# Block-sparse attention with a gated FFN: a plan computed while building against a written-out order of all pieces

## The chip, the core and the metric

The program runs on one core of one Trainium2 chip. The metric is device time in microseconds; three runs of the kernel before gave 344.5 to 351.38 with a median of 347.37. One more execution was profiled. Engines are named as in the profile: PE (TensorE matmuls), PEld (its weight loads), DVE (VectorE), ACT (ScalarE), POOL (GpSimd) and SP (SyncE, which here only issues DMAs and reads registers). POOL issues DMAs too, on a queue of its own.

## The reference

Attention with 4 batches, 8 heads, 768 positions of 64 numbers, cut into 24 blocks of 32 positions. A query block sees its neighbours, the first and the last block, and three blocks drawn for it (`sampled_blocks`); the first and last query blocks see everything. The output goes through a gated FFN with three matrices.

```python
mask = np.abs(blk_i - blk_j) <= 1
mask = mask | (blk_i == 0) | (blk_j == 0) | (blk_i == n_blocks - 1) | (blk_j == n_blocks - 1)
for qb in range(n_blocks):
    for kb in sampled_blocks[qb]:
        mask[qb*block:(qb+1)*block, kb*block:(kb+1)*block] = True
attn = softmax(np.where(mask, q @ k.T / sqrt(D), -1e9))     # per batch and head
x = (attn @ v).transpose(0, 2, 1, 3).reshape(B * S, H * D)  # 3072 x 512
out = (x @ w_gate -> sigmoid) * (x @ w_val) @ w_out         # d_ff = 1536, float32 out
```

## The kernel before, in words

**Pieces.** The kernel is a list of about 1400 pieces of a few instructions, each with an engine (or a choice of two), a duration, what it depends on, and the buffers that it takes and gives back. Names are a kind, the batch, and a number:

- `cdma`, `memset`, `mask`, `gv0`, `gc0`: constants, the block numbers, the mask row and the first and last block of batch 0's values.
- `ldv`, `ldk`, `ldq` (lines 564 to 579): loads of a batch's values, keys and queries by POOL's queue, converted to f16 on the way. In batch 0 the keys come in two halves (`ldk00`, `ldk01`), the queries in a first part of 64 rows and a second of 32 (`lda00`, `ldb00`).
- `trk`, `trq` with `evk`, `evq`: transposes of keys and queries on PE, and their copies out of PSUM. `rrk`, `rrq` (line 689) rearrange them on POOL first, from batch 1 on.
- `vsh` (line 738) rearranges the values on DVE, `scr` (746, 750) writes them to DRAM, and SP gathers from there: `w` (822) the neighbour blocks of a window of query blocks into V1A to V1D, `vg` (873) the three drawn blocks of one query block into V2A to V2D with three DMAs, whose addresses are registers. `regSP` and `regPOOL` (611) load these registers from `vidx` and `kidx`. `vfl` (787) fills the first and last block into the same buffers.
- `kfl` and `kg` (801, 858): POOL copies the fixed and the drawn key blocks together.
- For each pair of query blocks: `sc` (scores, 899 and 907), `mx` (row maximum, 917), `ex` (exponential, two halves, 927), `rz` (936), `sl` (normalisation, two halves: 948 on DVE or 945 on POOL), `tp` (transposes, 960), `te` (copy, 966), `pv` (probabilities by values, 978, and 983 in batch 0), `xe` (copy into the FFN's input). The first and last query blocks have the same with a `d` ahead: `dsc`, `dmx`, `dex`, `dsl`, `dtp`, `dte`, `dpv`, `dxe`.
- FFN, in nine groups of 1, 1, 2, 2, 2, 4, 4, 4 and 4 tiles of 128 tokens: for each of 12 slices `pg` and `pu` (gate and value matmuls, 1146), `th` (tanh, 1155), `h` (1160); then for each tile `py` (1173), `ys` (1182), `st` (the store). `wg`, `wv` and `wo` (589, 597) are the weights' loads on POOL's queue, in three chunks each: slices 0 to 3 need `wg0` and `wv0`, 4 to 7 `wg1` and `wv1`, the rest `wg2` and `wv2`.

**What sets the order.** `Planner.run` (from line 283) plays the pieces through on the durations given, takes at each step the piece with the lowest priority number among those that could start first, and gives it engine and buffers; `TUNE` holds the numbers, with some 180 offsets (`off`) by kind and batch. The order that comes out is the program's order, and each engine works through its own in that order. `sl` of batches 0 and 1 may only go to DVE, of batch 2 only to POOL, of batch 3 to either.

**Idle matmuls.** Until bank 7 of PSUM is first used, the emitting loop puts matmuls of zeros (WZ, line 1204) where the plan has PE waiting, as many as 0.9 of the planned gap holds. There are 91 of them.

**The start.** SP issues the block numbers, a table of block indices (`bb_cst`), the identity, and `gv0`. POOL clears WZ and other tiles, then issues the loads in the order `ldk00 ldk01 lda00 ldv00 ldb00 wg0 wv0`. DVE forms `kidx`, `vidx` and then the mask (13 more small instructions) as one piece, on which the register loads depend. PE begins with `trk000 ... trk003, trq000 ... trq003, dsc0_0, trq010 ... trq013, sc0_4, sc0_6`.

## Time and profile before

| | |
|---|---|
| median of three runs | 347.37 us |
| profiled execution | 350.14 us, span 348.3 us |
| PE busy | 323.6 us (93%), 65.3 us of it in line 1173, 25.6 us in idle matmuls (line 1204) |
| DVE, ACT, POOL busy | 239.0, 192.5, 130.5 us |
| granted clock of PE over the span | 0.985 |
| DMA | 42.26 MB in 43169 packets |

How to read it: "busy" is the time in which an engine had an instruction running; the ends of matmuls are modelled, and an idle matmul counts like any other. The granted clock is the share of full speed that PE was given. `SPq` and `POOLq` are the queues of instructions that issue DMAs or read registers. A row of the chain is start, length and what ran or was waited for; a row of a stretch is its bounds and length, then busy time and instructions by engine, the granted clock, the DMA engines' mean share and GB/s. A row of the order of time is start, length, engine, line, operation, and what wrote what; rows of DMA issues end with the size of each and the median us from issue to landing.

### The profile page before, as it was taken

What the parts mean: (1) busy time and instruction counts of PE and PEld (TensorE: products, weight loads), DVE (VectorE), ACT (ScalarE), POOL (GpSimd) and SP (SyncE); (2) the same over time, 40 slices, a digit from 0 to 9 for tenths busy, and PEclk for the clock granted to TensorE, in tenths of its full rate; (3) what the DMA queues carried; (4) which work ended last, traced back from release to release, by engine and by line L of the source; (5) the groups of instructions that cost most, each with busy time, mean ns of one, the idle gap of its engine ahead of it and who ended that gap; (6) DMA issues with size and microseconds to landing.
All of it is one profiled execution on the core that took longest, in us unless ns stands there. A gap on an engine that the chain in (4) does not pass through costs nothing.

```text
span 348.3 us, 13695 instructions
## 1 busy us (share of the span) xinstructions
PE 323.6 (93%) x5227; PEld 205.9 (59%) x5227; DVE 239.0 (69%) x516; ACT 192.5 (55%) x588; POOL 130.5 (37%) x364
## 2 busy tenths in 40 slices
PE   8979669699989989689999999999999999999995
PEld 3446448586767678378565665665556555544442
DVE  4788568661798979469998788587777679703320
ACT  2464356524676577377676554665774667424321
POOL 7946115104304434234827894465241222000000
PEclk9999998979999999999999999999999999999999
DMA  7987983997331359952349943531313412020002
GB/s 125 207 193 146 242 193 73 213 219 159 118 103 44 117 115 202 203 178 79 83 135 206 212 115 94 161 106 47 89 31 121 139 49 81 14 90 30 2 30 90
DMA packets 43169, 42.26 MB, mean 121 GB/s; under 512 B 6592, under 2 KB 39936, under 8 KB 43008
## 3 DMA queue, kind: packets, MB, share of 16 engines
q1 hardware_dynamic: 28912, 27.23, 25.9%
q0 software_dynamic: 14192, 14.16, 25.5%
q8 instruction: 41, 0.67, 0.8%
q14 instruction: 24, 0.20, 0.2%
HBM read 46.08 MB, written 9.44 MB: 159 GB/s over the span
## 4 chain that ended last, share of the span: by engine, by line
PE 64%; DMA 15%; DVE 9%; issue 3%; ACT 3%; SPq 3%; POOL 2%; POOLq 0%; DVEq 0%; ACTq 0%
PE pall L1146 29%; PE pall L1173 16%; DMA stg<-in_q_dram 5%; PE pall L960 4%; PE pall L978 4%; DMA stg<-in_v_dram 4%; SPq L873 3%; PE pall L907 2%; DMA V1D<-scr 2%; DVE HT L1160 2%; DVE NM L917 2%; DMA scr<-XL 2%; DVE P L948 2%; PE pall L899 2%; DMA V2D<-scr 2%
## 5 line engine op out<-in xcount | busy, mean ns | idle before, releaser
L927 ACT ACTIVATE P<-pall,NM 128x256 f16<-128x256 f32 x176 | 81.4, 473 | 18.5 <-DVE NM L917 14.7
L1160 DVE SCALAR_TENSOR_TENSOR HT<-TH,pall 128x512 f16<-128x512 f32 (+2 forms) x108 | 54.3, 505 | 46.0 <-PE pall L1146 41.2
L858 POOL COPY KG<-KT 128x64 f32 x264 | 50.8, 241 | 84.4 <-PE pall L907 80.3
L1155 ACT ACTIVATE TH<-pall 128x512 f32<-128x512 f32 (+2 forms) x108 | 48.8, 455 | 57.6 <-PE pall L1146 50.5
L1173 PE MATMUL pall<-wo,HT 128*128 128x512 f16 x288 | 65.3, 379 | 0.2
L917 DVE TENSOR_REDUCE NM<-pall 128x4 f32<-128x1024 f32 x44 | 53.6, 1220 | 12.7 <-PE pall L907 7.5
L1146 PE MATMUL pall<-XT,wv 128*128 128x256 f16 (+2 forms) x336 | 57.2, 295 | 2.1 <-DVE HT L1160 1.4
L1146 PE MATMUL pall<-XT,wg 128*128 128x256 f16 (+2 forms) x336 | 56.8, 293 | 1.2 <-DVE HT L1160 1.0
L1146 PEld LDWEIGHTS <-wv 128*128 128x128 f16 x432 | 38.3, 101 | 25.7 <-issue 4.2
L1146 PEld LDWEIGHTS <-wg 128*128 128x128 f16 x432 | 38.3, 100 | 23.9 <-issue 2.8
L1173 PEld LDWEIGHTS <-HT 128*128 128x128 f16 x288 | 27.4, 98 | 31.0 <-issue 1.1
L945 POOL TENSOR_TENSOR P<-P,ZZ 128x512 f16<-128x512 f16 x26 | 27.7, 1080 | 23.8 <-DVE ZZ L936 18.5
L927 ACT ACTIVATION_READ_ACCUMULATOR P<-pall,NM 128x1 f32 x176 | 36.2, 206 | 0.0
L948 DVE TENSOR_SCALAR P<-P,ZZ 128x256 f16<-128x256 f16 x124 | 32.6, 324 | 1.1
L1182 ACT ACTIVATE YS<-pall 128x512 f32<-128x512 f32 x16 | 9.6, 597 | 36.2 <-PE pall L1173 36.2
L966 DVE COPY PTS<-pall 128x1024 f16<-128x1024 f16 x39 | 26.6, 684 | 3.1 <-PE pall L960 3.0
L960 PE MATMUL pall<-ident,P 128*128 128x128 f16 x352 | 27.5, 223 | 0.6 <-DVE P L948 0.6
L1204 PE MATMUL pall<-WZ 128*128 128x512 f16 x91 | 25.6, 416 | 1.3 <-POOL ones L538 1.3
L960 PEld LDWEIGHTS <-P 128*128 128x128 f16 x352 | 22.4, 100 | 5.0 <-DVE P L948 0.8
L1146 PE MATMUL pall<-XL,wg 128*128 128x512 f16 x96 | 24.5, 379 | 0.1
L1146 PE MATMUL pall<-XL,wv 128*128 128x512 f16 x96 | 24.5, 379 | 0.0
L689 POOL COPY stg<-stg 96x2048 f32<-96x2048 f32 x6 | 11.3, 1889 | 28.4 <-DMA stg<-in_k_dram 21.5
(115 smaller groups left out, 443.9 us busy)
## 6 DMA issues: line engine op xcount, KB each, us to landing
out_dram<-YS SPq DMA_DIRECT2D x24, 256.0 KB, 2.0
stg<-in_v_dram POOLq DMA_DIRECT2D x4, 768.0 KB, 11.4
V2C<-scr SPq DMA_DIRECT2D x96, 32.0 KB, 3.1
V2D<-scr SPq DMA_DIRECT2D x78, 32.0 KB, 2.8
stg<-in_k_dram POOLq DMA_DIRECT2D x3, 768.0 KB, 12.4
stg<-in_q_dram POOLq DMA_DIRECT2D x3, 768.0 KB, 16.9
scr<-stg SPq DMA_DIRECT2D x12, 192.0 KB
V1C<-scr SPq DMA_DIRECT2D x5, 384.0 KB, 3.5
```

Of the source, the lines that this page charges most:

```text
L858: pin(nc.gpsimd.tensor_copy(t[:, :, u, (2 + n) * BLK : (3 + n) * BLK].bitcast(f32), KT[r].bitcast(f32)[:, :, bass.ds(regs[key][i, n], BLK ...
L917: pin(nc.vector.tensor_reduce(NM[o.slots[hz][1]][:, 0:4].rearrange("p (h u) -> p h u", h=2), t, axis=AX.X, op=ALU.max, negate=True))
L927: pin(nc.scalar.activation(pb[:, hh, u, :], t[:, hh, u * 256 : u * 256 + 256], AF.Exp, bias=NM[z][:, 2 * hh + u : 2 * hh + u + 1], scale=1 ...
L945: pin(nc.gpsimd.tensor_tensor(pb, pb, z[:, 2 * hh : 2 * hh + 2].unsqueeze(2).broadcast_to([128, 2, 256]), op=ALU.mult))
L948: pin(nc.vector.tensor_scalar(pb[:, u, :], in0=pb[:, u, :], scalar1=z[:, 2 * hh + u : 2 * hh + u + 1], scalar2=None, op0=ALU.mult))
L960: pin(nc.tensor.transpose(t[:, m * 128 : m * 128 + 128], pb[:, hh, u, c * 128 : c * 128 + 128], ident))
L966: pin(copy(o)(PTS[pl.handles[hTS][1]].rearrange("p m n -> p (m n)"), banks[pl.handles[hT][1]].bitcast(f16)))
L1146: pin(nc.tensor.matmul(t, wt[:, c, f_ * 128 : f_ * 128 + 128], XT[g][:, c, :], start=(c == 0), stop=(c == 3)))
L1155: pin(nc.scalar.activation(TH[o.slots[ht][1]][:, 0:n], banks[pl.handles[hg][1]][:, 0:n], AF.Tanh, bias=0.0, scale=0.5))
L1160: pin(nc.vector.scalar_tensor_tensor(HT[:, f_, hoff : hoff + n], in0=TH[pl.handles[ht][1]][:, 0:n], scalar=1.0, in1=banks[pl.handles[hv][1 ...
L1173: pin(nc.tensor.matmul(t, HT[:, f_, hoff + tt * 128 : hoff + tt * 128 + 128], wo[:, f_, :], start=(f_ == 0), stop=(f_ == NF - 1)))
L1204: pin(nc.tensor.matmul(banks[7], WZ[:, 0:128], WZ, start=True, stop=True))
```

## The change

1. `Planner.run` no longer plans: it reads a table, `ORDER`, in which every piece stands once, with its engine, the number of the buffer that it takes, and, behind a "+", the idle matmuls ahead of it. The offsets, margins and the 0.9 go; so do the planned gaps. There are 111 idle matmuls.
2. The table of block indices is counted by POOL (`iota`) in place of its DMA; WZ is cleared by DVE (`wz`) in place of POOL.
3. `kidx` and `vidx` are a piece of their own (`idx`), on which the register loads depend in place of `mask`. `gv0` is issued after `cdma`.
4. Batch 0 is loaded in the order values, two halves of keys, two parts of queries (`'first': 'vkab'`). `wg0` and `wv0` come after the first key gathers.
5. `sl` and `te` may go to either of two engines in every batch; the table says which. Durations of pieces are lower, which only the old planner read; names of the second part of the queries change (`trqb01...`).

The arithmetic of the other pieces is untouched.

```diff
- 'load': [4, 10, 7],
+ 'load': [17, 9, 9],
- 'gate': [-1, -1, 2, 3, 3, 6, 10, 13, 14],
+ 'gate': [-1, -1, 3, 3, 5, 5, 9, 9, 9],
- 'sl': ['D', 'D', 'P', 'PD'],
- 'te': ['D', 'DA', 'D', 'D'],
+ 'sl': ['PD', 'PD', 'PD', 'PD'],
+ 'te': ['DA', 'DA', 'DA', 'DA'],
- 'first': 'kavb',
+ 'first': 'vkab',
...
+ORDER = """
+wz:D memset:G cdma:S ldv00:G0 gv0:S ldk00:G3 ldk01:G lda00:G1 mask:D ldb00:G gc0:A vsh0:D0 vfl0D:D idx:D vfl0B:D
+regSP0_0:S regPOOL0_0:G trk001:P0+43 evk001:D scr0:S trk002:P0+7 trk000:P1 trk003:P3 evk000:A evk003:D evk002:A
+trq001:P0+5 kfl01:G trq000:P1 kfl00:G evq001:A trq002:P3 kg0_6:G1 evq000:A trq003:P2 evq002:D evq003:A kg0_4:G0
+sc0_6:P0+3 w0_4:S0 mx0_6:D1 vg0_6:S kfl02:G sc0_4:P3+1 kg0_8:G2 trqb011:P1 mx0_4:D6 ex0_60:A0 w0_8:S0 kg0_10:G0
+vg0_5:S ex0_61:A regPOOL0_1:G ex0_40:A1 rz0_6:D sc0_8:P0+9 sl0_61:D w0_16:S0 vg0_11:S mx0_8:D3 ex0_41:A wg0:G
+sc0_10:P3+5 rz0_4:D evqb011:D ex0_80:A2 wv0:G trqb012:P0 mx0_10:D5 vg0_7:S evqb012:A sl0_60:G trqb010:P0+2 sl0_41:D
+wg1:G tp0_6:P10+2 evqb010:D vg0_4:S vfl0A:D sl0_40:G ex0_100:A0 ex0_81:A kg0_12:G1 te0_6:A vfl0C:G sc0_12:P2+10
+trqb013:P0 ex0_101:A mx0_12:D2 tp0_4:P12 te0_4:D ex0_120:A1 vg0_8:S rz0_10:D rz0_8:D sl0_80:D sl0_81:G ex0_121:A
+dsc0_0:P02+6 dmx0_00:D0 w0_12:S0 sl0_100:G evqb013:A vg0_9:S pv0_4:P1+3 rz0_12:D dmx0_01:D7 dex0_00:A1 wv1:G
+tp0_8:P01 sl0_121:G te0_8:D xe0_4:A dex0_01:A0 pv0_6:P1+3 dsl0_00:D vg0_10:S kg0_18:G2 xe0_6:A dsl0_01:D
+dtp0_00:P00+2 sl0_101:D dsc0_23:P02 wg2:G dte0_00:D dtp0_01:P1 sl0_120:G dmx0_231:D4 dte0_01:A dmx0_230:D0 kg0_14:G0
+dex0_231:A1 tp0_12:P12+5 wv2:G dex0_230:A0 pg0_0:P00+1 pu0_0:P1 tp0_10:P00 wo0:G th0_0:A2 regSP0_1:S dsl0_230:D
...
+"""
...
-    ENG = ("PE", "ACT", "DVE", "POOL", "SP")
+    ENG = {"P": "PE", "A": "ACT", "D": "DVE", "G": "POOL", "S": "SP"}
-    def run(self, switch=0.095, dma_lat={"SP": 1.8, "POOL": 2.8}):
...
+    def run(self, table):
+        byname = {o.name: o for o in self.ops}
+        self.handles, self.whole = {}, {}
         order = []
+        for item in table.split():
+            item, _, idle = item.partition("+")
+            name, _, how = item.partition(":")
+            o = byname.pop(name)
+            o.eng, o.idle = self.ENG[how[0]], int(idle or 0)
+            for (h, options), c in zip(o.acq, how[1:]):
+                o.got[h] = self.whole[h] = options[int(c)]
+                o.slots[h] = self.handles[h] = options[int(c)][0]
...
             order.append(o)
...
-        pin(nc.sync.dma_start(cst_t, cst_h.ap()))
         pin(nc.sync.dma_start(ident, ident_h.ap()))
+    def f_wz(o):
+        pin(nc.vector.memset(WZ, 0.0))
     def f_memset0(o):
-        pin(nc.gpsimd.memset(WZ, 0.0))
         pin(nc.gpsimd.memset(ones, 1.0))
+        pin(nc.gpsimd.iota(cst_t, pattern=[[1, NB], [0, 3]], base=0, channel_multiplier=0, allow_small_or_imprecise_dtypes=True))
         pin(nc.gpsimd.memset(mrow, 0.0))
...
+    P("wz", "DVE", 0.3, f_wz, prio=-200)
+    def f_idx(o):
+        for t, n in ((vidx, BLK), (kidx, BLK // 2)):
+            pin(nc.vector.tensor_scalar(t, in0=flat[0:1], scalar1=n, scalar2=None, op0=ALU.mult))
     def f_mask(o):
-        pin(V.tensor_scalar(kidx, in0=flat[0:1], scalar1=BLK // 2, scalar2=None, op0=ALU.mult))
-        pin(V.tensor_scalar(vidx, in0=flat[0:1], scalar1=BLK, scalar2=None, op0=ALU.mult))
         pin(V.tensor_copy(rb.rearrange("p a b -> p (a b)"), flat))
...
+    o_idx = P("idx", "DVE", 0.3, f_idx, deps=[c_dma], prio=-101)
-                regop[key] = P(f"reg{eng}{b}_{part}", eng, 1.6, f_regs(eng, key, part), deps=[o_mask] + lastuse[eng], prio=pr - 3)
+                regop[key] = P(f"reg{eng}{b}_{part}", eng, 1.6, f_regs(eng, key, part), deps=[o_idx] + lastuse[eng], prio=pr - 3)
...
-    order = pl.run()
-        if warm and o.eng == "PE":
-            n = int((o.start - t_pe) * TUNE["warm"] / 0.2135)
-            for _ in range(n):
-                pin(nc.tensor.matmul(banks[7], WZ[:, 0:128], WZ, start=True, stop=True))
+    for o in pl.run(ORDER):
+        for _ in range(o.idle):
+            pin(nc.tensor.matmul(banks[7], WZ[:, 0:128], WZ, start=True, stop=True))
         if o.fn is not None:
             o.fn(o)
```

The rest of the table, as far as it is spoken of: of the pieces `sl1` it puts 15 of 22 on POOL, of `sl0` 11, of `sl2` 12, of `sl3` 10. POOL's order after the part shown is `wo0 kg0_16 regPOOL0_2 kg0_2 wo1 kg0_20 wo2 kg0_1 sl0_141 ldv10`, and around batch 2's queries `sl1_101 kg1_16 sl1_81 sl1_80 ldq20 kg1_18 ... rrq2`. On PE the second output tile `py1_0` comes after all eight transposes of batch 1 and `dsc1_0`; before, it came ahead of them. `trq201`, the first transpose of batch 2's queries, stands between `pg4_8` and `pg4_9`; `tp1_8` stands ahead of `py3_1`. In the last two groups the slices no longer run from 0 to 11 (`pg7_2 pg7_0 pg7_3 pg7_5 ...`, `pg8_8 pg8_1 pg8_9 ...`).

## The prediction

> **What bounds the kernel now.** I read the page's head first, then busy time over five stretches, then the idle matmuls (line 1204) in the same stretches. The stretches end where the first FFN matmul starts (40.5 us, second fence below), after the second output tile (85.1), where PE becomes full (179.8), and with the last matmul (344.7).

> ```profile
> span 348.3 us, 13695 instructions
> PE 323.6 (93%) x5227; PEld 205.9 (59%) x5227; DVE 239.0 (69%) x516; ACT 192.5 (55%) x588; POOL 130.5 (37%) x364
> ...
> core 0: us, PE busy (x) PEld busy (x) DVE busy (x) ACT busy (x) POOL busy (x), PEclk, DMA share, GB/s
> 0.00:40.50 40.50, 34.02 (x657) 18.58 (x658) 27.05 (x57) 18.56 (x52) 25.35 (x77) 1.00 0.94 176
> 40.50:85.10 44.60, 37.95 (x778) 29.91 (x777) 27.83 (x83) 21.24 (x84) 12.19 (x27) 0.89 0.92 181
> 85.10:179.80 94.70, 86.88 (x1674) 65.88 (x1672) 77.40 (x179) 62.77 (x182) 37.02 (x119) 1.00 0.49 124
> 179.80:344.70 164.90, 164.70 (x2125) 91.55 (x2122) 106.70 (x199) 89.37 (x269) 55.98 (x143) 1.00 0.34 91
> ...
> 0.00:40.50 40.50, 21.75 (x81) 7.71 (x81) 1.00 0.94 176
> 40.50:85.10 44.60, 3.90 (x12) 0.99 (x10) 0.89 0.92 181
> ```

> "93% busy" hides the start. In stretch 1 PE did 34.02 − 21.75 = 12.3 us of its own work in 40.5 us. In stretch 2 it lost 3.90 us to idle matmuls, 6.65 us to idling and, at a granted clock of 0.89, some 0.11 × 44.6 = 4.9 us: 15.5 us. In stretch 3 it idled 7.8 us while DVE was 82% busy. In stretch 4 it idled 0.2 us: nothing is to be had there, and the PE work of the program does not change. So the change can win only in the first 180 us.

> The chain that ended last says what the first stretches wait for:

> ```profile
> 3.79 12.97 DMA stg<-in_v_dram
> 16.79 1.29 DVE XL L738
> 18.09 6.78 DMA scr<-XL
> 24.89 0.33 SPq L822
> ...
> 33.75 8.16 DMA V1D<-scr
> 44.89 5.90 DMA V2D<-scr
> 50.83 0.54 PE pall L983 x9
> 66.12 2.61 issue
> 131.05 16.89 DMA stg<-in_q_dram
> ```

> Up to 50.8 us the kernel hangs on batch 0's values: loaded (the fourth load of the queue, landed at 16.8), rearranged, written to DRAM, gathered back block by block by SP. Later a hole follows the load of batch 2's queries (131 to 148).

> **The start, part by part.** The rows that carry it:

> ```profile
> 1.27 0.20 POOL L539 MEMSET mrow<- 128x120 bf16 x1
> 1.33 7.04 PE L1204 MATMUL pall<-WZ 128*128 128x512 f16 x20 [1.33 <-POOL ones L538]
> 1.59 1.52 POOL L575 DMA_DIRECT2D stg<-in_k_dram  x2
> 7.92 1.55 DVE L787 COPY V1D<-GV 32x2048 f16<-32x2048 f16 x1
> 8.96 1.40 POOL L787 COPY V2C<-GV 32x1024 f32<-32x1024 f32 x1
> 9.10 1.25 PE L1204 MATMUL pall<-WZ 128*128 128x512 f16 x5
> 15.23 1.53 PE L1034 MATMUL pall<-KT,QT 64*32 64x384 f16 x16
> 25.41 8.29 SPq L873 DMA_DIRECT2D V2C<-scr  x12
> 27.09 1.19 PE L1093 MATMUL pall<-DPT,XL 96*64 96x32 f16 x64
> 28.21 2.12 PE L1204 MATMUL pall<-WZ 128*128 128x512 f16 x9
> 32.26 0.62 PE L960 MATMUL pall<-ident,P 128*128 128x128 f16 x8
> 40.68 0.39 PE L1146 MATMUL pall<-XT,wg 128*128 128x128 f16 x4
> ...
> stg<-in_k_dram POOLq DMA_DIRECT2D x2, 384.0 KB, 6.1
> wv<-in_moe_w_val_dram POOLq DMA_DIRECT2D x1, 512.0 KB, 7.7
> ...
> L611 SPq TENSOR_LOAD <-vidx x16: 747/1430/2873, 4.8 to 276.1; - x16
> ```

> *Counting indices on GpSimd.* A DMA of constants goes (0.42 us of SP, under which nothing waits), an iota comes ahead of the first load on POOL, and the clearing of WZ leaves POOL for DVE. No row shows an iota of 128 × 72 numbers: between 0 (it might cost less than the clearing of WZ that left) and 1.40 us (a POOL copy of far more); I take 0.2 us, by the nearest row, the clearing of mrow. What it costs delays every load.

> *Values first.* They have the bytes of the two key halves together, whose second was issued at about 2.4 us and landed 6.1 us later by the median: I take 9 us instead of 16.8. But SP does not profit by all of it. In the written order SP's scr0 (the write to DRAM) stands behind regSP0_0, the register loads, which wait for the two products of idx, and DVE has vsh0 (1.29), then vfl0D (two copies of 1.4 to 1.6), then idx (0.4). So scr0 goes out at 9 + 1.3 + 3.0 + 0.4 + 1.4 (the median TENSOR_LOAD) = 15.1 us against 18.1: a wait is added with scr0 behind it, and all the gathers behind scr0. Three us are won of the 7.8. The write took 6.78 us beside the first two weight loads; these move back behind the first key gathers, but the loads of keys and queries take their place, so I leave 6.8: landed at 21.9.

> *The first gathers.* SP's order now needs 18 DMAs (w0_4, vg0_6, w0_8, vg0_5, w0_16, vg0_11, vg0_7, vg0_4) before the first P·V, where it was 13, the number that took from 24.89 to 33.70: 0.68 us each. At 0.5 us (the pace without stalls, 1.5 us per three) they are out at 30.9, at 0.68 at 34.1. With 3 to 5 us to land, pv0_4 can start between 34 and 39.

> *PE's own order.* The idle matmuls are now numbers in the list: 107 stand ahead of pg0_0. The first 20 took 7.04 us, further ones (2.12 − 1.25)/4 = 0.218 us: 7.04 + 87 × 0.218 = 26.0 us. Real work ahead of pg0_0 is the 12.3 us of before, less dpv0_0 (1.19), plus tp0_12 (0.62) and dsc0_23 (1.53): 13.3. From 1.3 us that gives 40.6, what it was. The gathers' path gives 34 to 39 plus what follows pv0_4 (11 idle matmuls, 2.4, and about 3.8 of pieces) = 40.4 to 45. I take **42 us: 1.5 lost**; ends −0.2 and 4.5.

> **Stretch 2.** By 42 us SP has 18 of batch 0's gathers behind it and no further wait on a landing write; the next ten (vg0_8, w0_12, vg0_9, vg0_10) are out by 31 to 34 + 5 to 7 and landed by about 43, where the old chain had V2D landing at 50.8. The four idle matmuls left cost 0.9 in place of 3.9: 3.0 won. Of the idling, the issue stall of 2.61 us waits for no data and may come back; the other 4.0 is won. Of the lost clock I keep what follows such a stall, half: 2.4 won. Sum **9.4 us**; ends 0 and 15.5. What is late next are the weights: their loads now stand on POOL behind key gathers and normalisations.

> **Stretch 3.** The knob that gave all of batch 1's normalisations to DVE goes; the list puts 15 of 22 halves of sl1 on POOL, 12 of batch 2's and 10 of batch 3's, and 11 of batch 0's.

> ```profile
> 40.50:85.10 44.60, 7.26 (x32) 0.89 0.92 181
> 85.10:179.80 94.70, 12.67 (x44) 1.00 0.49 124
> 179.80:344.70 164.90, 9.92 (x36) 1.00 0.34 91
> ...
> 85.10:179.80 94.70, 2.31 (x2) 1.00 0.49 124
> ...
> L945 POOL TENSOR_TENSOR P<-P,ZZ 128x512 f16<-128x512 f16 x26 | 27.7, 1080 | 23.8 <-DVE ZZ L936 18.5
> L1146 PE MATMUL pall<-XT,wv 128*128 128x256 f16 x141 | 21.4, 273 | 1.5 <-DVE HT L1160 1.0 <-ACT TH L1155 0.5
> ```

> (The first three rows are the DVE normalisations of line 948 in stretches 2 to 4, the fourth POOL's of line 945 in stretch 3; the other 24 of its 26 lie in stretch 4.) A half is two instructions, 12.67/44 × 2 = 0.58 us on DVE; 15 of them are 8.6 us off an engine at 82%, for 15 × 1.08 = 16.2 us on POOL, which was busy 37.0 of 94.7. Batch 2's query load is issued some 18 us of PE work ahead of its first transpose (between tp1_8 and trq201), as long as the 16.9 us it took. I take **8.6 us won**; the ends are 0 (POOL's half takes 0.5 us longer and lies in the chain of each unit) and 20: the 7.8 idle and the drawn-out FFN matmuls: 21.4/141 = 0.152 us each for wv, as many for wg, against 0.108, half of a 512-column one in stretch 4 (1.73/8 = 0.216): 282 × 0.044 = 12.4 us.

> ```profile
> 244.14 1.73 PE pall L1146 x8
> ```

> [...]

> **Stretch 4 and the end** are left: PE is full, the last output tile, its copy and its store stay (3.6 us). The written order shuffles groups 7 and 8; 0, with ±2.

> **Sum.** Span 348.3 + 1.5 − 9.4 − 8.6 = 331.8; the profiled execution took 350.14, 1.8 more than its span, and stands 2.8 above the median of 347.37. Against the median: 347.4 − 16.5 = **331 us**.

> **Rivals.**
> - *DVE's relief is void* (0.14). [...]
> - *The start wins nothing* (0.11). Loads share the 16 engines, so values land hardly sooner, keys and queries later, and the fixed idle matmuls only add to waits. Stretch 2 keeps its 15.5: 331 + 9.4 = 340. Against it: the keys landed 6.1 us after issue, the values, two loads later in the queue, 12.97.
> - *Stretches 2 and 3 close almost fully* (0.08): 331 − 6 − 6 = 319.
> - *Slower: the weights come late* (0.07). wv1, wg2, wv2 stand on POOL behind sl0 halves that wait for the softmax, and vfl0C. A weight load lands 7.7 us after its issue (the row above); pg0_4 needs wv1 and pg0_8 wv2. Each us after about 45 (wv1) or 49 (wv2) is a us of PE. Gains of 16.5 are used up when wv2 lands at about 66; ten more, at 76, makes 357.
> - The forecast itself has 0.60, own range 324 to 338.

> A measurement here tells about 2% from no change: below 340.4 is faster, above 354.3 slower. Faster holds the forecast, the fast case, nearly all of the first rival and half of the second: 0.85; same 0.09; slower 0.06. The range leaves out one in ten at each side: 319 to 344.

> **What would show it.** scr0 issued near 15 us, not at 10 (then SP's registers did not hold it) and not at 18; pg0_0 at 40 to 45; the second output tile ending, with batch 1's transposes already done, at 77 to 79 instead of 85; DVE under 75% busy between there and the filling of PE; PE full from about 160. I am wrong if POOL's queue is seen waiting for softmax while weights stand behind it, or if DVE's copies grow longer.

## The result and the profile after

The changed kernel takes **357.35 us** (median; 357.06 to 357.73), the kernel before 348.18 in the same session: ratio 1.03, 95% interval 1.022 to 1.039. It is 9 us slower; the prediction had it 16 us faster. The profiled execution took 357.06 us.

First the page of the changed kernel (busy time; a DMA queue with packets, MB and share; the chain's shares), then the view by stretches, cut at the first FFN matmul (44.5), the end of the second output tile (92.0), the first piece of FFN group 5 (175.3) and the last matmul (351.6), then the idle matmuls (line 1019) in them:

```profile
span 355.3 us, 13665 instructions
...
PE 330.9 (93%) x5247; PEld 208.7 (59%) x5247; DVE 234.2 (66%) x474; ACT 199.8 (56%) x589; POOL 148.4 (42%) x384
...
q8 instruction: 41, 0.67, 0.8%
...
PE 70%; DVE 14%; issue 7%; ACT 6%; POOL 3%; POOLq 0%; DVEq 0%; ACTq 0%
```

```profile
core 0: us, PE busy (x) PEld busy (x) DVE busy (x) ACT busy (x) POOL busy (x), PEclk, DMA share, GB/s
0.00:44.50 44.50, 41.45 (x644) 20.67 (x645) 29.42 (x57) 21.16 (x61) 28.92 (x80) 1.00 0.98 193
44.50:92.00 47.50, 39.73 (x906) 32.08 (x907) 28.84 (x72) 25.66 (x87) 19.68 (x50) 0.89 0.78 145
92.00:175.30 83.30, 79.18 (x1480) 61.16 (x1480) 58.38 (x129) 55.90 (x167) 41.04 (x103) 0.98 0.57 130
175.30:351.60 176.30, 170.58 (x2234) 94.78 (x2224) 117.54 (x216) 96.44 (x276) 58.74 (x152) 1.00 0.32 89
...
0.00:44.50 44.50, 27.87 (x107) 9.96 (x107) 1.00 0.98 193
44.50:92.00 47.50, 1.35 (x4) 0.35 (x4) 0.89 0.78 145
```

In the prediction's own sums: ahead of the first FFN matmul PE loses 44.5 − (41.45 − 27.87) = 30.9 us (before 28.2); in stretch 2 1.35 of idle matmuls + 7.77 idling + 0.11 × 47.5 = 5.2 of clock = 14.3 (15.5); in stretch 3 it idles 4.1 us (7.8); in stretch 4 5.7 us (0.2). No transfer is left in the chain, which before hung on values, their write and their gathers up to 50.8 us. But the chain counts idle matmuls as work, and with 107 of them ahead the first FFN matmul still comes 4 us later than before (44.5 against 40.5). In place of the transfers stands "issue" with 7%, time in which PE waits for nothing that the profile shows. The chain in order of time (start, length, what) says where:

```profile
1.20 11.50 PE pall L1019 x43
...
51.17 2.14 issue
...
63.94 2.58 issue
...
72.41 2.36 issue
...
104.58 2.99 issue
...
175.41 2.69 PE pall L969 x12
```

Four stalls of over 2 us, 10.1 us together, where the kernel before had one put down to "issue" (66.12, 2.61).

A second measure needs no view. The written order says which records of PE belong to which piece, so two runs can be compared at points where PE has done exactly the same pieces. There is such a point just ahead of the changed kernel's first piece of group 5. PE reaches it at 175.3 us in the changed kernel and at 175.8 before. **Up to there the two profiled executions are level; from there to the last matmul the changed kernel takes 176.2 us, the old order 168.8.** That execution of the kernel before was a long one (350.14 us beside a median of 348.18), and two others of the old order, below, come to the point at 170.4 and 176.4. So "level" isn't settled: of the 9.2 us between the medians 7.4 lie behind the point, which leaves some 2 ahead of it, an estimate. Where an expectation speaks of lost time, it is the clock less the work done so far, each piece counted at a short duration usual for its kind.

### The profile page after: what moved, and what is told of

It reads as the page before. It is cut to its first block, busy times and chain, and to the rows that moved or that the text cites. A ratio compares the mean times of both kernels' runs of the same rounds, so it can differ in the third digit from the quotient of the medians.

```text
span 355.3 us, 13665 instructions
## 1 busy us (share of the span) xinstructions
PE 330.9 (93%) x5247; PEld 208.7 (59%) x5247; DVE 234.2 (66%) x474; ACT 199.8 (56%) x589; POOL 148.4 (42%) x384
## 4 chain that ended last, share of the span: by engine, by line
PE 70%; DVE 14%; issue 7%; ACT 6%; POOL 3%; POOLq 0%; DVEq 0%; ACTq 0%
PE pall L969 28%; PE pall L996 15%; PE pall L783 5%; PE pall L1019 4%; PE pall L801 4%; DVE NM L740 3%; DVE P L771 3%; DVE HT L983 3%; PE pall L730 2%; PE pall L528 2%; ACT P L750 2%; PE pall L891 2%; PE pall L722 2%; POOL KG L681 1%; PE pall L806 1%
## 5 line engine op out<-in xcount | busy, mean ns | idle before, releaser
L983 DVE SCALAR_TENSOR_TENSOR HT<-TH,pall 128x512 f16<-128x512 f32 (+2 forms) x108 | 53.7, 504 | 49.9 <-PE pall L969 34.0
L768 POOL TENSOR_TENSOR P<-P,ZZ 128x512 f16<-128x512 f16 x48 | 49.6, 1044 | 80.8 <-DVE ZZ L759 74.8
L969 PE MATMUL pall<-XT,wv 128*128 128x256 f16 (+2 forms) x336 | 58.0, 298 | 4.8 <-issue 3.0
L740 DVE TENSOR_REDUCE NM<-pall 128x4 f32<-128x1024 f32 x44 | 53.5, 1218 | 13.3 <-PE pall L730 8.7
L969 PE MATMUL pall<-XT,wg 128*128 128x256 f16 (+2 forms) x336 | 57.8, 297 | 3.0 <-issue 2.4
L771 DVE TENSOR_SCALAR P<-P,ZZ 128x256 f16<-128x256 f16 x80 | 30.3, 432 | 0.6
L1019 PE MATMUL pall<-WZ 128*128 128x512 f16 x111 | 29.2, 402 | 1.2 <-DVE WZ L352 1.2
L783 PE MATMUL pall<-ident,P 128*128 128x128 f16 x352 | 26.5, 219 | 1.7 <-DVE P L771 1.5
L789 DVE COPY PTS<-pall 128x1024 f16<-128x1024 f16 x27 | 18.4, 684 | 3.9 <-PE pall L783 3.9
L730 PE MATMUL pall<-KG,QT 64*32 64x160 f16 x704 | 20.2, 237 | 0.4 <-issue 0.2
L1003 DVE TENSOR_SCALAR YS<-pall 128x512 f32<-128x512 f32 x14 | 9.5, 682 | 15.7 <-PE pall L996 13.6
## 6 DMA issues: line engine op xcount, KB each, us to landing
V1C<-scr SPq DMA_DIRECT2D x5, 384.0 KB
```

What stands on the lines that cost most here:

```text
L730: pin(nc.tensor.matmul(t[32 * p : 32 * p + 32, hh, u * 256 + c0 : u * 256 + c1], QT[r][kp, p, i * BLK : (i + 1) * BLK], src, start=False, ...
L740: pin(nc.vector.tensor_reduce(NM[o.slots[hz][1]][:, 0:4].rearrange("p (h u) -> p h u", h=2), t, axis=AX.X, op=ALU.max, negate=True))
L768: pin(nc.gpsimd.tensor_tensor(pb, pb, z[:, 2 * hh : 2 * hh + 2].unsqueeze(2).broadcast_to([128, 2, 256]), op=ALU.mult))
L771: pin(nc.vector.tensor_scalar(pb[:, u, :], in0=pb[:, u, :], scalar1=z[:, 2 * hh + u : 2 * hh + u + 1], scalar2=None, op0=ALU.mult))
L783: pin(nc.tensor.transpose(t[:, m * 128 : m * 128 + 128], pb[:, hh, u, c * 128 : c * 128 + 128], ident))
L969: pin(nc.tensor.matmul(t, wt[:, c, f_ * 128 : f_ * 128 + 128], XT[g][:, c, :], start=(c == 0), stop=(c == 3)))
```

## Experiments

The changed kernel itself was timed once, beside 348.18 us for the kernel before. In the sessions of the runs below the kernel before took 346.6 to 347.7 us, and the ratios are to these. A difference from 357.35 us is therefore uncertain by 0.5 to 1.6 us.

**The old order in the new code.** Order, engines, buffers and idle matmuls of the kernel before, written out as a table:

```diff
-wz:D memset:G cdma:S ldv00:G0 gv0:S ldk00:G3 ldk01:G lda00:G1 mask:D
+memset:G wz:D cdma:S ldk00:G0 gv0:S ldk01:G lda00:G1 ldv00:G2 idx:D mask:D
...
```

> The order of the kernel before, written out piece by piece with its engines, buffers and idle matmuls, in the code of the changed kernel; so of the change only the first instructions are left (block numbers first, the block indices counted on POOL, the zeroing on DVE, the multiples ahead of the mask), and the loads go keys, queries, values as before. If the new order costs the 9 us: 345 to 350 us, as the kernel before. If one of the other parts costs them: 353 or more.

Measured: 346.71 us, ratio 1.0035 (0.9995 to 1.0076). Iota, zeroing on DVE, the separate index products and the planner's absence cost nothing and win nothing that can be seen within 1%. The 9 us lie in the order, with its engines and idle matmuls.

**Only the late part in the old order**, from the first piece of group 5 on:

```diff
 sc2_1:P2 dsl2_231:D
-pg5_0:P10 mx2_1:D0 w2_2:S0 vfl2A:G pu5_0:P0 th5_0:A0
+mx2_1:D2 ex2_10:A0 kg2_4:G0 w2_2:S0 ex2_11:A vg2_2:S
...
```

> The changed kernel's order up to the first piece of FFN group 5 (about 176 us), all pieces left over in the order of the kernel before. If the new order loses by itself after 176 us (holes of PE of 11.3 us there against 3.4 before): 349, between 347 and 351. If those holes come from something carried over from the first half, or from POOL's share beside DVE: 355 to 359.

Measured: 359.48 us, 1.038 (1.029 to 1.047), which answered neither. At the seam PE waits 7.01 us for a normalisation on POOL; there it stands behind fills of V buffers that wait for a gather of batch 2's values. From the common point to the seventh piece of group 5 this run needs 26.2 us, where both orders by themselves need 17.5 to 18.3. Behind the seam it ran as in the kernel before (151.37 us from the seventh piece of group 5 on, in both). Taken up again below.

**All normalisations on DVE.**

```diff
-sl0_60:G
+sl0_60:D
...
-sl3_160:G
+sl3_160:D
```

> The changed kernel with all 48 normalisation halves that POOL does given to DVE, the order as it is. Shared operands theory (POOL's tensor_tensor holds DVE up, 7.9 us in the normalisations, more in other copies): 352 or less, and DVE's normalisation half near 0.57 us everywhere. Order theory and instruction theory: no gain, 356 to 362, since DVE gets 48 times 0.57 us more.

Measured: 364.22 us, 1.053 (1.044 to 1.061). The groups by line (count, then busy us and mean ns), changed kernel first (L771 DVE, L768 POOL):

```profile
L768 POOL TENSOR_TENSOR P<-P,ZZ 128x512 f16<-128x512 f16 x48 | 49.6, 1044 | 80.8 <-DVE ZZ L759 74.8 <-PE pall L969 5.8
L771 DVE TENSOR_SCALAR P<-P,ZZ 128x256 f16<-128x256 f16 x80 | 30.3, 432 | 0.6
```

```profile
L769 DVE TENSOR_SCALAR P<-P,ZZ 128x256 f16<-128x256 f16 x176 | 46.6, 316 | 0.7
```

So the effect exists: DVE's instruction takes 432 ns in the mean with POOL's halves beside it and 316 without. Taken one by one, it took 0.28 us where nothing ran on POOL and 0.63 in the mean for the 23 of 80 that overlap a normalisation there. One place of the changed kernel, in order of time, shows it at its worst, two instructions, beside a normalisation and then two copies on POOL:

```profile
219.51 2.99 DVE L771 TENSOR_SCALAR P<-P,ZZ 128x256 f16<-128x256 f16 x2
219.54 1.04 POOL L768 TENSOR_TENSOR P<-P,ZZ 128x512 f16<-128x512 f16 x1 [3.46 <-DVE ZZ L759]
...
220.53 3.84 POOL L512 COPY stg<-stg 96x2048 f32<-96x2048 f32 x2
...
222.55 0.73 PE L783 MATMUL pall<-ident,P 128*128 128x128 f16 x10 [1.06 <-DVE P L771]
```

Why DVE's instruction takes longer there no run shows; shared operands were my assumption. But it isn't what costs the 9 us: without POOL's halves the program behind the common point takes 175.9 us instead of 176.2 (in an execution of 359.95), and DVE, with 16 us more of normalisations, makes the whole slower. This run alone could hide a relief behind that extra work; but the old order has 24 halves on POOL behind the common point, the new one 22, and still takes only 168.8 us there.

**PE's instructions moved by 64 matmuls.**

```diff
-trk001:P0+43
+trk001:P0+36
+        for _ in range(71 if o.name == "trk001" else 0):
+            pin(nc.tensor.matmul(banks[7][:, 0:8], WZ[:, 0:128], WZ[:, 0:8], start=True, stop=True))
```

> The changed kernel with 71 matmuls of 8 columns added and 7 idle ones of 512 columns left out ahead of the first transpose, so that the instruction stream of PE is 64 matmuls longer from there and the time of the start about the same. Theory that PE's four stalls by issue (51.2, 63.9, 72.4 and 104.6 us, 10.1 us in sum) are instruction blocks of about 127 matmuls that come late: the stalls leave dpv0_0, dpv0_23, group 1's fifth tile and group 2's sixth, and stand 64 matmuls earlier in the program or are gone; the time goes anywhere from 349 to 359. Theory that they belong to what is computed there: they stay at those pieces with 2.1 to 3.0 us each, 356 to 358.

Measured: 352.43 us, 1.017 (1.010 to 1.024): 4.9 us less for 64 useless matmuls more. The stalls leave their pieces and become 2.48, 2.72, 0.76 and 1.09 us. Number of matmuls started from 0 up to each stall, changed kernel, then this one, then the kernel before (the second column of numbers is PE's busy time, x its matmuls):

```profile
0.00:51.10 51.10, 48.05 (x859) 1.00 1.01 196
0.00:63.90 63.90, 58.72 (x1115) 0.95 1.02 195
0.00:72.40 72.40, 64.63 (x1242) 0.93 1.01 189
0.00:104.50 104.50, 93.12 (x1876) 0.95 0.83 162
```

```profile
0.00:49.25 49.25, 46.70 (x859) 1.00 1.00 194
0.00:55.30 55.30, 50.27 (x987) 0.99 1.02 197
0.00:75.50 75.50, 67.61 (x1369) 0.93 0.96 180
0.00:105.20 105.20, 95.45 (x2004) 0.95 0.86 167
```

```profile
0.00:66.10 66.10, 55.97 (x1240) 0.97 0.88 171
```

859, 987, 1115, 1242, 1369, 1876, 2004: they lie 127 or 128 apart, or a multiple of it, in both kernels, whatever is computed there; the one of the kernel before, at 1240, is two short of 1242. Had they belonged to pieces, the second kernel's would stand at 923, 1179, 1306 and 1940. And the page counts 41 packets of 0.67 MB in the queue "instruction": 16 KB each, for 2 × 5247 matmuls and weight loads, 256 to a packet. From these counts I read such a stall as a block of instructions that comes late, at one of the borders that lie about 127 matmuls apart. The packets of the trace bear this out. The four that are missing start at 50.99, 64.15, 72.38 and 105.20 us and take 0.93 to 0.97 us, and PE goes on 1.4 us after each. By then PE had used up what it had, or all but one matmul (858, 1115, 1242 and 1876 started). Packets that come in time start earlier: those for the borders near 1369, 1496, 1623 and 1750 at 1292, 1411, 1498 and 1621, when PE is at most 50 matmuls into the block ahead, the one for the border near 987 at 959.

**Smaller loads.** What makes it late? Ahead of each of the four late packets the DMA engines' share (last but one) is 1.20 to 1.26; here each row ends where the packet starts (PE's busy time, its clock, the share, GB/s). While PE then stands, it can be far lower (0.31 from 64 to 66 us). The share alone doesn't settle it: from 34 to 36 us it is 1.22, and the packet that starts there, at 35.48 us, came 88 matmuls ahead of its border near 605.

```profile
48.50:51.00 2.50, 2.50 (x110) 1.00 1.24 229
62.00:64.15 2.15, 1.94 (x71) 1.00 1.25 211
70.00:72.40 2.40, 2.40 (x70) 0.95 1.26 214
102.00:105.20 3.20, 2.58 (x91) 1.00 1.20 194
```

The loads issued last before them are weights (at 47.26 and 50.30), the values of batch 1 (57.98), its keys and queries (64.79 and 65.60), and the values of batch 2 (99.51). The row of the loads of values among the DMA issues (size of each, median us from issue to landing):

```profile
stg<-in_v_dram POOLq DMA_DIRECT2D x4, 768.0 KB, 8.1
```

```diff
+        if f"{name}{b}" in ("v1", "k1", "q1", "v2"):
+            parts = [(0, TP, 0, 1)]
```

> The changed kernel, but of the values, keys and queries of batch 1 and of the values of batch 2 only one head of eight is transferred (so the output of those batches is not the reference's; all else is done in full). Theory that blocks of PE's instructions come late because they stand in the DMA engines behind these loads: the stalls by issue at 63.9, 72.4 and 104.6 us (7.9 us) go, and the lower clock behind them too; the one at 51.2 us stays, since the weights still land then; 345 to 350 us. Theory that transfers have nothing to do with it: the stalls stay and the time is 355 or more.

Two pieces, `ldq10` and `vsh1`, also exchange their staging buffers in this run.

Measured: 347.44 us, 1.0017 (0.998 to 1.006): 9.9 us less. The stretches around the last three stalls, changed kernel first (columns as in the first view by stretches):

```profile
60.00:70.00 10.00, 7.41 (x194) 6.54 (x193) 4.30 (x14) 6.17 (x25) 3.60 (x4) 0.84 0.91 138
70.00:80.00 10.00, 7.64 (x147) 5.69 (x145) 7.49 (x19) 3.53 (x15) 0.88 (x1) 0.99 0.67 118
100.00:110.00 10.00, 6.60 (x218) 5.20 (x215) 5.54 (x15) 5.24 (x21) 1.23 (x7) 0.89 0.76 146
110.00:120.00 10.00, 10.00 (x125) 7.81 (x124) 6.11 (x18) 7.39 (x23) 7.60 (x19) 0.94 0.21 61
```

```profile
60.00:70.00 10.00, 9.86 (x308) 8.66 (x306) 7.39 (x23) 7.12 (x29) 3.11 (x4) 1.00 0.17 26
100.00:110.00 10.00, 10.00 (x131) 8.04 (x131) 6.98 (x19) 7.50 (x24) 8.51 (x23) 1.00 0.32 93
```

The three stalls are gone, and so is the lower clock around them (0.84, 0.89 and 0.94 of full speed become 1.00). The first stays, 2.08 us at the same place, with the weights landing. So without the data of these 768 KB loads the blocks came in time. Some of the 9.9 us may be ordinary relief of transfers, which this run cannot split off; the next ones leave nothing out.

**The old start, then the new order**, with keys first up to the first FFN piece:

```diff
-wz:D memset:G cdma:S ldv00:G0 gv0:S ldk00:G3 ldk01:G lda00:G1 mask:D
+memset:G wz:D cdma:S ldk00:G0 gv0:S ldk01:G lda00:G1 ldv00:G2 idx:D mask:D
...
 pg0_0:P00+1 pu0_0:P1
```

> Up to the first FFN piece the order of the kernel before (keys, queries, values), then all pieces left over in the changed kernel's order. If the start with values first costs time (PE's lost time by 40 us is 30.0 in the changed kernel, 26.6 in the old order under the new first instructions): 351 to 355 us. If what the start wins or loses is made up later: 356 to 359. The instruction stream is 24 matmuls shorter ahead of the first FFN piece, so the stalls by issue may lie elsewhere; their sum is to be read beside the time.

Measured: 353.11 us, 1.022 (1.015 to 1.029): 4.2 us less. In the profiled execution (348.60 us; the other three took 353.0 to 355.3) one stall by issue of over 2 us is left on PE, 2.60 us at matmul 1876 again; a gap of 1.89 us at matmul 1115, which the profile puts down to a gather, lies on a border too. PE reaches the common point at 167.2, not 175.3, and then takes 176.0. An earlier point with the same pieces done, behind `dpv0_0`, it passes at 50.0 us, and the two spliced kernels below that start alike at 53.3 and 51.6; values first, the changed kernel and seven others pass it at 53.6 to 54.8. So the start with values first costs, but waits of about 2 us lie ahead of that point in most of these runs: how much of the 4.2 is the start itself and how much fewer stalls isn't separated.

**One part alone: 15 halves of batch 1 on POOL**, in the old order.

```diff
-sl1_10:D
+sl1_10:G
...
-sl1_181:D
+sl1_181:G
```

> The old order in the new code (346.7 us) with one part of the change alone: the same 15 normalisation halves of batch 1 from DVE to POOL as in the changed kernel. The prediction's term for the third stretch (8.6 us won by taking them off DVE): 338 to 341 us. Rival, that DVE is not what ends PE's waits there: 345 to 349. Rival, that POOL's normalisation holds up DVE and the key gathers behind it: 350 or more.

Measured: 348.99 us, 1.0052 (1.001 to 1.009), beside 1.0035 for the old order without it: nothing won. The stretch from 83 us of the old order in the new code, then that from 85 us of this run (it starts that much later):

```profile
83.00:176.00 93.00, 85.83 (x1639) 65.68 (x1632) 78.49 (x181) 63.00 (x186) 39.19 (x123) 1.00 0.50 123
```

```profile
85.00:178.50 93.50, 84.72 (x1573) 63.83 (x1558) 68.21 (x143) 60.21 (x178) 52.90 (x131) 0.98 0.49 121
```

DVE was relieved as reckoned, from 78.5 to 68.2 us, and PE was no busier. Between two points with the same pieces done, behind the changed kernel's `pg3_6` and ahead of its group 5, this run needs 48.5 us, the old order 46.1 (46.8 in the code before) and the changed kernel 42.5.

**The end in the old order**, from group 7 on:

```diff
 sc3_10:P2 te3_6:A
-pg7_2:P61 mx3_10:D2 pv3_6:P1 rz3_8:D pu7_2:P2 sl3_80:D
+vg3_8:S st6_2:S pg7_0:P10 st6_3:S th7_0:A0 pu7_0:P0 rz3_8:D
...
```

> The changed kernel's order up to the first piece of group 7 (277 us), the rest in the order of the kernel before, whose next pieces are the same ones, so that there is no seam. From there PE loses 4.6 us in the changed kernel and 1.7 in the one before. If the new order's end is at fault: 353.5 to 355. If the holes come from what is carried over: 356.5 to 358.

Measured: 354.85 us, 1.025 (1.018 to 1.032): 2.5 us less. From the last common point ahead of group 7 to the last matmul the new order takes 75.5 us, the old one 72.3, and this run 72.3: 3.2 us are the new order's end.

**One load moved.**

```diff
-pu2_3:P0 pg2_4:P10 ldv20:G1 ex1_10:A2 dpv1_0:P0
+pu2_3:P0 pg2_4:P10 ex1_10:A2 dpv1_0:P0
...
-pg3_0:P00 h2_11:D vfl1D:G tp1_2:P01
+pg3_0:P00 h2_11:D ldv20:G1 vfl1D:G tp1_2:P01
```

> The changed kernel with one piece moved: the transfer of the values of batch 2, issued at 99.5 us so far, is issued behind the start of an instruction block that runs for 9.8 us (about 115 us). Theory of late instruction blocks: the stall at matmul 1876 (104.6 us, 2.99 us) goes, with the lower clock behind it (0.89 and 0.94 from 100 to 120 us); the three before it stay; 352 to 354.5 us. Rival, that the stall is bound to another cause there: 356.5 to 358.

Measured: 353.48 us, 1.025 (1.019 to 1.030): 3.9 us less, inside the forecast. In the profiled execution 0.61 us is left of the 2.99 at matmul 1876. That execution was the fastest (349.38; the others 353.5 to 355.9), and the stalls at 1115 and 1242 are missing in it too, which this edit doesn't explain. The other three have no trace, so which stalls they kept isn't known; that a block comes in time in one execution and late in another is an estimate from these times.

**Three corrections at once**: old start, new middle with that load moved, old end; the edits of the three runs above, and nothing else.

> Three corrections at once: the old order up to the first FFN piece, the changed kernel's order from there to group 7, the old order to the end, and the transfer of the values of batch 2 moved as in the run with that alone. If the three gains add up (4.2 of the start, 2.5 of the end, 2.6 of the stall at 97.9 us left in the run with the old start): 343.5 to 347, so no slower than the kernel before. If the stalls come back elsewhere: 349 to 354.

Measured: 345.24 us, 0.9939 (0.990 to 0.998): 0.6% under the kernel before, and 12.1 us under the changed one. The three gains forecast make 9.3, so they add up.

**Two weight loads later**, on top of it:

```diff
-ldb00:G wg0:G gc0:A wv0:G vfl0C:G
+ldb00:G gc0:A vfl0C:G
...
-kg0_6:G1 vsh0:D0 kg0_8:G2
+kg0_6:G1 vsh0:D0 wg0:G wv0:G kg0_8:G2
```

> The same with the first two weight transfers issued behind the second key gather (about 22 us) instead of behind the queries at 5 us. Theory: the stall by issue near 22 us (1.1 to 2.1 us, where the second weight transfer lands at 24.6) goes, and the first V rows land sooner: 1.5 to 3 us less than the run without it. Rival: the weights then stand in the way of the gathered V rows from 24 to 34 us, no gain or up to 3 us more.

Measured: 347.39 us, 1.0053 (1.002 to 1.008), 2.2 us more. The stall stayed (1.86 us at 22.9), and two more by issue came, 2.24 us at matmul 860 and 1.71 at 1115 (there the run without this edit has 1.82, put down to a gather). The first FFN matmul comes at 47.3 us, not 44.9. The time is the rival's; that the weights stand in the way of the V rows isn't shown apart from the late blocks.

**The old order from 194 us on**, at a point with the same pieces done, in the changed kernel and in the corrected one:

```diff
 vg2_4:S ex2_60:A2
-pg5_6:P10 xe2_1:D ex2_61:A pv2_2:P0 h5_5:D st4_1:S tp2_20:P12
+st4_1:S xe2_1:A vg2_5:S vg2_7:S ldq30:G2 regPOOL2_1:G scr3:S kg2_12:G1 pg5_6:P10
...
```

> The changed kernel's order up to the seventh piece of FFN group 5 (194 us), the rest in the order of the kernel before. At this point PE has done exactly the same pieces in both orders, so the seam is smaller than in the first such run. From there PE loses 9.8 us in the changed kernel and 3.2 in the one before. If the new order itself makes the holes after 194 us: 350 to 353. If they come from what is carried over from the first half: 355.5 to 358. If the seam (the queries of batch 3 are transferred later in the new order) costs as much as in the first run of this kind: 357 to 361.

> The spliced kernel of 345.24 us, but the old order already from that same piece at 194 us on, not from group 7. If the holes from 194 to 277 us belong to the new order: 341 to 343.5. If not, or if the seam costs them again: 345 to 350.

Measured: 355.22 us, 1.026 (1.023 to 1.029), 2.1 us less than the changed kernel; and **343.82 us**, 0.992 (0.989 to 0.996), the fastest kernel here, though not told apart from 345.24. Both lie between the ranges forecast. The gain was smaller, because the seam takes part of it back: up to the last common point ahead of group 7 these runs need 81.5 and 80.9 us from the seam, the new order 82.5, the old one in its own run 79.1.

Together, from the profiled executions:

| kernel | profiled execution (median) | common point reached | from there to the last matmul |
|---|---|---|---|
| before | 350.14 (348.18) | 175.8 | 168.8 |
| changed | 357.06 (357.35) | 175.3 | 176.2 |
| old order, new code | 344.61 (346.71) | 170.4 | 168.8 |
| old order, 15 halves on POOL | 351.13 (348.99) | 176.4 | 169.0 |
| all normalisations on DVE | 359.95 (364.22) | 178.6 | 175.9 |
| shifted by 64 matmuls | 352.93 (352.43) | 171.1 | 176.2 |
| smaller loads | 347.68 (347.44) | 165.3 | 176.9 |
| old start, new order | 348.60 (353.11) | 167.2 | 176.0 |
| load moved | 349.38 (353.48) | 167.7 | 176.2 |
| old end | 354.93 (354.85) | 175.9 | 173.6 |
| three corrections | 345.41 (345.24) | 167.2 | 172.8 |
| two weight loads later, with the corrections | 348.25 (347.39) | 170.0 | 172.8 |
| old order from 194 | 353.13 (355.22) | 175.5 | 172.1 |
| old order from 194, with the corrections | 345.60 (343.82) | 167.8 | 172.3 |

The right column depends on the order behind the point alone, within about 1 us, whatever came before and with or without POOL's normalisations. So 7.4 us of the loss are the new order behind 175 us: 0.8 up to 194 us, 3.5 from there to group 7 and 3.2 after it. The left column goes with the late blocks. Counting PE's waits by issue of over 1.6 us between 45 us and the point, the new order gets there at 165 to 168 us with one or none (five runs), at 170 to 171 with two (two runs), and at 175 to 179 with three or four (four runs). The old order isn't explained by that: it gets there at 170.4, 175.8 and 176.4 with one such wait at most.

## Why the prediction was wrong

- **Start (1.5 lost).** The working held: the write of the values went out at 14.1 us, not at 15.1 (row below), the first FFN matmul came at 44.5, in the range of 40.4 to 45 but above the 42 taken; 2.7 us were lost. Idle matmuls, 27.87 us for 107, were longer than the 26.0 summed.

```profile
L569 SPq DMA_DIRECT2D scr<-XL x1: 338/338/338, 14.1 to 14.1; - x1
```

- **Stretch 2 (9.4 won): this step failed.** 1.2 us came. The idle matmuls went as summed (1.35 us left). The 4.0 us of idling that were to go did not: it rose from 6.65 to 7.77. The 2.4 us of clock did not come either (5.2 lost, 4.9 before). The prediction wrote of the single stall that it "waits for no data and may come back", and counted it once. There were three in this stretch, 7.1 us, and the clock fell behind two of them. I had read "issue" as an accident of one place. Behind these stalls is the queue of instruction blocks, with a row on the page that I had not used (41 packets here), and a change that issues loads at other times or crosses the borders at other times moves them: 0.61 us for 2.99 with one load moved, 2.48, 2.72, 0.76 and 1.09 us at other pieces with the borders moved. I also looked for what is late next among data, and named the weights; they were issued in time (the last at 50.3 us).
- **Stretch 3 (8.6 won): some gain came, for another reason.** The changed kernel idled 3.7 us less there, with a stall of 2.99 in it; in the kernel with three corrections, without that stall, PE idled 1.5 us of 84.6 (row below), 6.3 less than before, though these stretches do not hold the same pieces. Between the two points with the same pieces done (behind `pg3_6` and ahead of group 5) the new order wins 3.6 to 4.3 us: 42.5 for 46.1 and 46.8. But the relief of DVE that the step rested on won nothing by itself. DVE was 70% busy there (58.38 of 83.3 us), as foretold, and was not what set PE's pace in the old order (its own run: nothing won); the gain belongs to the new order of that stretch as a whole, and which of its moves brings it wasn't tried.

```profile
90.00:174.60 84.60, 83.11 (x1577) 63.06 (x1575) 63.46 (x135) 60.45 (x183) 47.52 (x116) 1.00 0.58 137
```

- **Stretch 4 (0 ± 2): this step failed too.** "PE is full" described the old order; the new list orders those pieces anew, and nothing kept them full. Behind the common point PE idles 5.7 us of 176.3, where the old order idles 0.5 of 168.9: eleven holes of 0.2 to 1.1 us, behind DVE and ACT for the most part, like that at 222.55 above. The other 2.2 of the 7.4 us are busy time (170.6 for 168.4), which isn't explained. The last hole is the plainest: the list makes the first row of the hidden values last, and the output tile that reads it first must wait (changed kernel, in order of time):

```profile
340.29 0.69 DVE L983 SCALAR_TENSOR_TENSOR HT<-TH,pall 128x512 f16<-128x512 f32 x1 [1.04 <-PE pall L969]
341.04 3.63 PE L996 MATMUL pall<-wo,HT 128*128 128x512 f16 x16 [0.85 <-DVE HT L983]
```

- **Rivals.** "The start wins nothing" was the nearest in mechanism, "DVE's relief is void" (stretch 3 as before, 331 + 8.6 = 339.5 us) true of the part: with 15 halves on POOL DVE fell from 78.5 to 68.2 us and nothing was won. The slower case was given to late weights; it came from late instructions and a looser second half, and neither was among the rivals. That its sum could make 357 us is chance. In the kernel before the means of line 948 show nothing of POOL's normalisations (12.67/44 = 0.288 us with two of them in stretch 3, 9.92/36 = 0.276 with 24 in stretch 4), but the five of its instructions that overlapped a normalisation on POOL took 0.66 us each, 0.29 where POOL was idle.

What a stall costs can be read twice: 3.9 us by the median where the load ahead of the stall of 2.99 was moved (2.3, if each kernel is set against the kernel before of its own session), and 9.9 (9.4) for three stalls of 7.9 together where loads were cut, both with the clock that falls behind them.

## What to carry to other kernels

Where the chain shows "issue" on PE, count the matmuls up to it: if the counts of several such stalls differ by multiples of some 127, look whether the packets of the queue "instruction" start only when PE has run out, and at what share of the DMA engines (1.20 to 1.26 here). Here moving a large load, or the border, won 4 to 5 us by the medians. A stretch that is full under one order need not be so under another (0.2 us idle of 164.9 before, 5.7 of 176.3 here): a new list must be followed there piece by piece, and two runs are best compared where they have done the same pieces. Try one part alone before adding its gain: here DVE, busy 78.5 of 93.0 us, was relieved by 10 us with nothing won.
